# Three low halves of W2 written by an adding DMA, and four key casts moved to GpSimd

## The chip, the cores and the metric

The kernel runs on one core of one Trainium2 chip. The metric is the device time of one execution in microseconds (us); the median of three runs before the change is 792.12 us, the lowest 791.73 and the highest 793.36. The engines are called PE (TensorE, matrix products), DVE (VectorE), ACT (ScalarE), POOL (GpSimd) and SP (SyncE, which issues most DMAs). Each works through its own list of instructions in order; an instruction that must wait holds up all that stand behind it on its engine.

## The reference

Block-sparse attention is followed by layer norm and a two-layer network with a residual:

```
scores = q @ k.T / 8                     # 4 batches, 8 heads, 768 positions, 64 per head
scores = where(mask, scores, -1e9)       # mask from blocks of 32: window, edges, sampled blocks
attn   = softmax(scores) @ v
x      = attn, heads side by side        # (4, 768, 512)
xn     = (x - mean) / sqrt(var + 1e-6) * g
out    = x + relu(xn @ W1) @ W2          # W1 512 x 2048, W2 2048 x 512, given as float64
```

## The kernel before

All large products are done in fp16 with each operand split into a high half (the value rounded to fp16) and a low half (what the rounding left, again in fp16). A product is then three: high by high, high by low, low by high. So whatever PE reads has first to be cast (high half) and subtracted (low half) by other engines.

The work goes in 12 units, each a third of a batch (256 positions); a unit has four pairs of heads, so there are 48 segments and 96 score groups of 12 matmuls (function `scores`, L602). Per segment follow the masked maxima on DVE (L611, in pairs), the exponentials on ACT (L625), the normalised high half `ph` on ACT (L688) and its low half `pl` on DVE (L692, after a reciprocal pair L677 and L679), their transposition by DMA, and the product with `v` (L728 to L737). Per unit follow the layer norm (its last step is `xl`, the low half of the normed values, L877), the first layer's 192 products with `w1h`, `w1l` and the second layer's 192 with `w2h`, `w2l` (both in `product`, L313), and the stores: `ot` on DVE (L932), which also frees the bank of accumulators, and an output DMA. The products of the network serve as filler: PE takes them in a fixed order, in between the score groups and the products with `v`. Only in unit 0 does the second layer go chunk by chunk of W2, two banks side by side, since W2 is still being unpacked.

W1 comes in 8 chunks and W2 in 16; `(2, 15)` is W2's last chunk. `loads_w` (L482) handles one chunk: a DMA brings the float64 bits into a raw buffer (W2's last chunks share two buffers, `raw0` and `raw1`, with the raw keys); DVE puts an fp32 number together from them in three steps (`first` L529, `second` L533, `third` L537, or L542 with POOL's addition L547); ACT scales it (L565) and casts the high half (L571); then the low half is made, by POOL's `tensor_sub` (L577), or by DVE for the chunks in LOWDVE (L579). `loads_k` (L351) handles the keys of a pair of heads: DMA L360, cast to the high half `kh` on ACT (L370), low half `kl` on DVE for the first 12 of 16 and on POOL for the last four (L363). `loads_q` copies queries by a DMA that POOL issues (L397), and POOL makes their low half (L400).

The order of each engine's instructions is set by the class `Plan`: every piece of work is a task with an engine, an assumed cost, tasks it comes after, a rank, and buffers it takes and gives back. `run` builds the lists greedily from these numbers, and `lock` keeps DVE's and POOL's tasks apart in its reckoning (on the chip nothing keeps them apart but the semaphores). A changed task can thus change the order of everything planned later.

Of the kernel before, what the change touches and what calls it, by code (L numbers as in the profile page):

```python
# [13 lines left out]
AF = mybir.ActivationFunctionType  # L14
ALU = mybir.AluOpType
# [161 lines left out]
def sparse_attention_moe(  # L177
# [12 lines left out]
    nc = tc.nc  # L190
# [31 lines left out]
    HIGHAT, LOWAT = -3.61, 0.01  # L222
# [2 lines left out]
    LOWDVE = ((2, 2), (1, 1), (2, 11), (1, 7), (2, 4), (2, 6), (2, 3), (1, 0), (2, 9), (2, 13), (1, 6), (1, 2))  # L225
    AVHOLD = 4
    KEEP = 90000.0
    CASTK, CASTQ = 16, 5
    MASKAT = 11.99
    KAT, VAT, QAT = 4.32, 10.55, 11.84  # L230
# [20 lines left out]
    def queue_of(kind):  # L251

        return (nc.gpsimd, "POOL", 900) if kind in POOLQ else (nc.sync, "SP", 580)

    plan = Plan()
    plan.span, plan.hot, plan.cold, plan.deep = 3400.0, 0.85, 0.4, 7000.0
    plan.keep, plan.first = KEEP, 1400.0
    plan.mode, plan.plain = None, PLAIN
# [92 lines left out]
    def loads_k(b, pr, rank, before):  # L351
        idx = b * NPAIR + pr
        o = SimpleNamespace()
        qk = "k" if b else ""

        def raw():
            o.kh = kvp.tile([P, S], F16, tag="kh", name=f"kh{idx}")
            o.kl = kvp.tile([P, S], F16, tag="kl", name=f"kl{idx}")
            o.kr = raw_s[RAWS.index(plan.where("raw", ("k", idx)))][:, 0:S]
            queue_of(qk)[0].dma_start(o.kr, ks[b, pr])  # L360

        def low():
            (nc.vector if idx < KDVE else nc.gpsimd).tensor_sub(o.kl, o.kr, o.kh)  # L363

        o.raw = plan.add(*queue_of(qk)[1:], raw, (before,), rank, 2000, load=1120, order="k",
                         take=(("k", idx), ("raw", ("k", idx), 2 if idx < RAWS_S else 1, RAWS)))
        if idx < RAWS_S:
            rank = 4 * pr + SPLITAT
        if idx < CASTK:
            o.high = plan.add("ACT", 730, lambda: nc.scalar.copy(o.kh, o.kr), (o.raw,), rank)  # L370
        else:
            o.high = plan.add("POOL", 560, lambda: nc.gpsimd.dma_start(o.kh, ks[b, pr]),
                              (o.raw,), rank, 2300, load=1500, order="k")
        e, x = ("DVE", 870) if idx < KDVE else ("POOL", 1640)
        o.low = plan.add(e, x, low, (o.raw, o.high), rank, give=(("raw", ("k", idx)),), lock=True)
        return o
# [105 lines left out]
    def loads_w(kind, i, before, w1done, low_tail):  # L482

        o = SimpleNamespace()
        own = (kind, i)
        qw = "w" if kind == 2 else ""
        if kind == 1:
            fs = slice(i * 2 * P, (i + 1) * 2 * P)
            rank = W1AT[i]
            scale, size, name = SW1, 1.0, "w1"  # L490
            stage = ("hh", "hl")[i] if i < 2 else "w1raw"
            take = ((stage, own),)
        else:
            rank = W2AT[i]
            scale, size, name = SW2, 0.5, "w2"
            stage = "raw"
# [53 lines left out]
        if kind == 2 and i >= 10:  # L550
# [3 lines left out]
            load=2900 * size, take=take, order="w")  # L554
# [20 lines left out]
        def low():  # L575
            if own not in LOWDVE:
                nc.gpsimd.tensor_sub(o.dl, o.src, o.dh)  # L577
            else:
                nc.vector.scalar_tensor_tensor(out=o.dl, in0=o.src, scalar=left, in1=o.dh,  # L579
                                               op0=ALU.mult, op1=ALU.subtract)  # L580

        if own in HIDMA and own in PORC:
            o.high = plan.add("POOL", 560, lambda: nc.gpsimd.dma_start(o.dh, o.src), (d,), rank + HIGHAT,
                              4300, load=2270 * size)
        else:
            o.high = plan.add("ACT", 940 * size + 60, high, (d,), rank + HIGHAT)
        e, x = ("DVE", 1135 * size + 35) if own in LOWDVE else ("POOL", 2020 * size + 140)
        o.low = plan.add(e, x, low, (o.high,), rank + LOWAT, lock=True,
            give=((stage, own),) + ((("wf", own),) if kind == 1 else ()))
# [411 lines left out]
    for rank, kind, x, pr in sorted(order):  # L1001
        if kind == 0:
            kt[x, pr] = loads_k(x, pr, rank, lk)
            lk = kt[x, pr].raw
        elif kind == 1:
            qt[x] = loads_q(x, rank, lq)
            lq = qt[x].raw
            if x == 0:
                iota = plan.add("POOL", 350, lambda: nc.gpsimd.affine_select(
                    ident, ident, pattern=[[-1, P]], compare_op=ALU.not_equal, fill=1.0, base=0,  # L1010
                    channel_multiplier=1), (qt[0].raw,), -5)
        else:
            vt[x, pr] = loads_v(x, pr, rank, lv)
            lv = vt[x, pr].last
# [4 lines left out]
    for i in range(FP):  # L1019
        wo1.append(loads_w(1, i, lw, (), ()))  # L1020
        lw = wo1[-1].load
        if i == 0:
            lw.after += [kt[0, 0].raw, qt[0].raw]
            for x in lw.after[-2:]:
                x.next.append(lw)
                lw.left += 1
    for i in range(FT):
        tails = [x.low for x in wo2[:10]] if i >= 10 else ()
        wo2.append(loads_w(2, i, lw, [x.low for x in wo1], tails))
        lw = wo2[-1].load  # L1030
# [3 lines left out]
    for seg in segs:  # L1034
# [4 lines left out]
        for t in range(TS):  # L1039
            a, b = pair = seg.slots[2 * t : 2 * t + 2]  # L1040
            give, whole = (), seg.i < RAWS_S
            if t == TS - 1:
                give = ((("qr", seg.i), ("raw", ("k", pr))) if whole else (("q", seg.i),)) + ((("k", u.b * NPAIR + pr),)
                                          if LAST[u.b, pr] is seg else ())
# [26 lines left out]
        if seg.early and (seg.i + NPAIR >= len(segs) or not segs[seg.i + NPAIR].early):  # L1071
            rank = seg.slots[0].i + UPS + 1
# [9 lines left out]
    for seg in segs:  # L1082
        n = 2 * seg.i + AVHOLD
# [71 lines left out]
```

## Time and profile before

| | |
|---|---|
| median of three runs | 792.12 us |
| span of the profiled execution | 790.0 us |
| busy: PE | 778.1 us (98%) |
| busy: DVE | 621.5 us (79%) |
| busy: ACT | 509.4 us (64%) |
| busy: POOL | 105.2 us (13%) |
| last matrix product begins | 786.28 us |

The span runs from the first to the last event that the profiler saw on the core; the run's own time is a little longer than the span. No other time of the profiled execution is given. Shares are averages over stages with different limits, so the stretch in question has to be looked at by itself. The profile's timelines give start, length, engine, line, operation, what it writes and reads, and, in brackets, how long the engine sat idle before it and for what.

### The profile page before, as it was taken

To read this page: it belongs to the slowest core of one execution; us is meant where nothing else is said; L and a number is where in the kernel's file an instruction comes from. 1 tells how busy PE (TensorE), PEld (TensorE's weight loads), DVE (VectorE), ACT (ScalarE), POOL (GpSimd) and SP (SyncE) were. 2 spreads that over 40 slices of the span, in tenths; PEclk is the share of its full clock that TensorE was granted. 3 is DMA by queue.
4 is the path that set the end of the run, shared out by engine and by line. 5 is a ranking of instruction groups with operands and counts; after the bars stand their busy time and mean duration, and the time that the engine had idled before them with its cause. 6 is when DMAs were issued, how large, how long until landed. Compare 5 with 4: busy or idle time off the path is not lost.

```text
span 790.0 us, 18464 instructions
## 1 busy us (share of the span) xinstructions
PE 778.1 (98%) x7336; PEld 600.0 (76%) x7336; DVE 621.5 (79%) x1225; ACT 509.4 (64%) x948; POOL 105.2 (13%) x117
## 2 busy tenths in 40 slices
PE   8999999999999999999999999999999999999998
PEld 5655677778777777777777777777777777788887
DVE  6989999988988788989878878888877878854220
ACT  6888876687666667777766766667656657652110
POOL 0444332200101000001011012021000100000000
PEclk9999999999999999999999999999999999999999
DMA  9553545978977688998785787887766656561000
GB/s 324 181 147 109 161 135 153 231 161 164 165 134 129 139 128 162 169 192 157 144 135 124 132 163 132 172 166 156 137 131 112 140 118 110 121 122 25 21 1 27
DMA packets 285638, 109.27 MB, mean 138 GB/s; under 512 B 253808, under 2 KB 277360, under 8 KB 285552
## 3 DMA queue, kind: packets, MB, share of 16 engines
q1 hardware_dynamic: 278544, 104.91, 61.1%
q0 software_dynamic: 6720, 3.08, 3.5%
q8 instruction: 57, 0.93, 0.5%
q14 instruction: 29, 0.24, 0.1%
q10 hardware_dynamic: 288, 0.10, 0.1%
HBM read 42.97 MB, written 6.29 MB: 62 GB/s over the span
## 4 chain that ended last, share of the span: by engine, by line
PE 89%; DVE 6%; ACT 2%; DMA 1%; issue 1%; SPq 1%; POOL 0%; ACTq 0%
PE bank L313 65%; PE ps L602 11%; PE pa L732 7%; PE pa L737 3%; PE pa L728 1%; DVE p L611 1%; DMA w1r<-w 1%; PE bank L640 1%; DVE w2h L533 1%; ACT pt L647 1%; DVE w2h L529 0%; DVE allow L328 0%; DVE w2h L537 0%; ACT p L625 0%; POOL w2h L547 0%
## 5 line engine op out<-in xcount | busy, mean ns | idle before, releaser
L313 PE MATMUL bank<-hh,w2h 128*128 128x256 f16 x768 | 204.5, 273 | 0.0
L313 PE MATMUL bank<-hh,w2l 128*128 128x256 f16 x768 | 204.1, 273 | 0.0
L313 PE MATMUL bank<-hl,w2h 128*128 128x256 f16 x768 | 204.1, 273 | 0.0
L611 DVE CUSTOM_DVE_ANT_1 p<-ps,allow 128x768 f32<-128x768 f32 x184 | 170.1, 951 | 24.0 <-PE ps L602 23.8
L625 ACT ACTIVATE p<-p,st 128x768 f32<-128x768 f32 x184 | 170.5, 928 | 15.7 <-DVE st L611 15.5
L313 PEld LDWEIGHTS <-w2h 128*128 128x128 f16 x1536 | 147.4, 98 | 25.8 <-issue 8.9
L313 PEld LDWEIGHTS <-w1h 128*128 128x128 f16 x1536 | 148.7, 98 | 23.6 <-issue 6.7
L313 PE MATMUL bank<-xh,w1h 128*128 128x256 f16 x768 | 115.4, 273 | 1.4 <-ACT pt L647 1.4
L313 PE MATMUL bank<-xh,w1l 128*128 128x256 f16 x768 | 115.4, 273 | 0.0
L313 PE MATMUL bank<-xl,w1h 128*128 128x256 f16 x768 | 115.3, 273 | 0.0
L916 DVE SCALAR_TENSOR_TENSOR hl<-bank,hh 128x512 f16<-128x512 f32 x96 | 66.2, 689 | 48.5 <-ACT hh L910 47.7
L910 ACT ACTIVATE hh<-bank 128x512 f16<-128x512 f32 x96 | 57.0, 594 | 65.4 <-PE bank L313 64.7
L688 ACT ACTIVATE ph<-p,st 128x768 f16<-128x768 f32 x92 | 83.5, 927 | 19.6 <-issue 8.2
L692 DVE SCALAR_TENSOR_TENSOR pl<-p,st,ph 128x768 f16<-128x768 f32 x92 | 94.3, 1042 | 1.2 <-DMA pt<-pl 1.0
L313 PEld LDWEIGHTS <-w1l 128*128 128x128 f16 x768 | 73.3, 98 | 13.7 <-issue 5.5
L313 PEld LDWEIGHTS <-w2l 128*128 128x128 f16 x768 | 75.0, 98 | 8.9 <-issue 0.2
L732 PE MATMUL pa<-pt,vh 128*64 128x512 f16 x468 | 79.2, 383 | 0.0
L688 ACT ACTIVATE raw<-p,st 128x768 f16<-128x768 f32 x64 | 57.9, 928 | 25.6 <-issue 14.7
L397 POOL DMA_DIRECT2D qh<-q x43 | 24.6, 571 | 333.7 <-PE ps L602 299.7
L692 DVE SCALAR_TENSOR_TENSOR raw<-p,st,raw 128x768 f16<-128x768 f32 x64 | 67.0, 1062 | 0.0
L602 PE MATMUL ps<-kh,qh 64*128 64x512 f16 (+1 forms) x376 | 64.9, 328 | 0.6 <-DVE st L611 0.5
L737 PE MATMUL pa<-pt,vl 128*64 128x256 f16 x468 | 64.6, 273 | 0.0
(125 smaller groups left out, 986.7 us busy)
## 6 DMA issues: line engine op xcount, KB each, us to landing
qr<-q SPq DMA_DIRECT2D x48, 128.0 KB, 3.0
raw<-k SPq DMA_DIRECT2D x16, 384.0 KB, 3.9
vr<-v SPq DMA_DIRECT2D x32, 192.0 KB, 2.9
out<-ot SPq DMA_DIRECT2D x48, 128.0 KB, 1.9
raw<-w SPq DMA_DIRECT2D x11, 512.0 KB, 3.8
w2l<-w SPq DMA_DIRECT2D x4, 1024.0 KB, 8.0
qh<-q POOLq DMA_DIRECT2D x43, 64.0 KB, 3.0
w1r<-w SPq DMA_DIRECT2D x2, 1024.0 KB, 8.3
```

What stands on the lines that cost most here:

```text
L313: nc.tensor.matmul(dst, w, x, start=start, stop=stop, skip_group_check=True)
L397: o.high = plan.add("POOL", 560, lambda: nc.gpsimd.dma_start(o.qh, qs[u.b, pr, u.c]), (o.raw,), rank, 2300, load=600, order="q")
L533: nc.vector.scalar_tensor_tensor(out=o.wf, in0=o.raw[:, :, 1], scalar=-0x40000000, in1=o.wf, op0=ALU.bitwise_and, op1=ALU.bitwise_or)
L602: nc.tensor.matmul(s.ps[:, lo:hi], x[rows, s.qs], y[rows, lo:hi], start=n == 0, stop=n == len(terms) - 1)
L611: nc.vector.tensor_tensor_reduce(out=s.p.rearrange(blk, k=BLK), in0=s.ps[:, 0:S].rearrange(blk, k=BLK), in1=bias, scale=-0.125, scalar=3.0 ...
L625: nc.scalar.activation(s.p, s.p, AF.Exp, bias=s.st[:, j : j + 1], scale=-1.0, accum_out=total)
L688: nc.scalar.activation(s.ph, s.p, AF.Copy, scale=s.r)
L692: nc.vector.scalar_tensor_tensor(out=s.pl, in0=s.p, scalar=s.r, in1=s.ph, op0=ALU.mult, op1=ALU.subtract)
L732: nc.tensor.matmul(seg.pa[half[hh], 0 : 2 * CH], vo.vh[:, hh, t, :], pts[keys[hh]][:, t].rearrange("p i n -> p (i n)"), start=t == 0, stop ...
L737: nc.tensor.matmul(seg.pa[half[hh], 0:CH], vo.vl[:, hh, t, :], pts[keys[hh]][:, t, 0, :], start=False, stop=t == KT - 1, skip_group_check= ...
L910: nc.scalar.activation(u.hh[:, f : f + 2, :].rearrange("p f n -> p (f n)"), bank[plan.where("bank", own)], AF.Relu)
L916: nc.vector.scalar_tensor_tensor(out=u.hl[:, f : f + 2, :].rearrange("p f n -> p (f n)"), in0=bank[plan.where("bank", own)], scalar=0.0, i ...
```

## The change

For three chunks of W2 the low half is made in another way. Before, it was one subtraction, fp32 value minus high half. Now an engine first writes the negated high half into the low half's place (chunk 5: DVE, chunk 14: POOL, chunk 15: ACT), and then a DMA that POOL issues adds the fp32 chunk onto it. And the keys of the last batch (numbers 12 to 15) are cast to their high half by POOL's copy, where ACT did it.

```diff
+    LOWDMA = {(2, 5): "DVE", (2, 14): "POOL", (2, 15): "ACT"}
+    CASTPOOL = 12
...
-        if idx < CASTK:
+        if idx >= CASTPOOL:
+            o.high = plan.add("POOL", 1000, lambda: nc.gpsimd.tensor_copy(o.kh, o.kr), (o.raw,), rank,
+                              lock=True)
+        elif idx < CASTK:
             o.high = plan.add("ACT", 730, lambda: nc.scalar.copy(o.kh, o.kr), (o.raw,), rank)
...
+        def minus():
+            if LOWDMA[own] == "ACT":
+                nc.scalar.activation(o.dl, o.dh, AF.Copy, scale=-1.0)
+            elif LOWDMA[own] == "DVE":
+                nc.vector.tensor_scalar(out=o.dl, in0=o.dh, scalar1=-1.0, scalar2=None,
+                                        op0=ALU.mult)
+            else:
+                nc.gpsimd.tensor_scalar(out=o.dl, in0=o.dh, scalar1=-1.0, scalar2=1.0,
+                                        op0=ALU.mult, op1=ALU.mult)
...
+        if own in LOWDMA:
+            e = LOWDMA[own]
+            n = plan.add(e, {"DVE": 400, "ACT": 1000, "POOL": 1200}[e] * size, minus, (o.high,),
+                         rank + LOWAT, lock=e != "ACT")
+            o.low = plan.add("POOL", 560, lambda: nc.gpsimd.dma_start(o.dl, o.src, accum_op=ALU.add),
+                             (n,), rank + LOWAT, 4300, load=2270 * size, give=((stage, own),))
+            return o
```

Because the tasks and their assumed costs differ, the plan puts the work in another order from about 100 us on. Line numbers grow by 5 up to `loads_w` and by up to 22 behind it.

On POOL, the two subtractions of chunks 14 and 15 (the third and fourth row here; the first is that of an earlier chunk), before:

```order
L577 TENSOR_TENSOR w2l<-raw_116,w2h 128x512 [waits Activation_49]
L397 DMA qh_1835<-q 128x256 [waits PE_49]
L577 TENSOR_TENSOR w2l<-raw_116,w2h 128x512 [waits Activation_49]
L577 TENSOR_TENSOR w2l<-raw_115,w2h 128x512 [waits Activation_49]
L400 TENSOR_TENSOR ql_118<-qr_1834,qh_1835 128x256 [waits DMAHW2_49,DMASW2_49,PE_49]
```

and the same place in the changed kernel, where L594 is the negation for chunk 14 and the two rows L606 are the adding DMAs of chunks 14 and 15:

```order
L402 DMA qh_1821<-q 128x256 [waits PE_49]
L594 TENSOR_SCALAR w2l<-w2h 128x512 [waits Activation_49]
L405 TENSOR_TENSOR ql_118<-qr_1820,qh_1821 128x256 [waits DMAHW0_49,DMASW3_49,PE_49]
L606 DMA w2l<-raw_115 128x512 [waits Pool_49]
L606 DMA w2l<-raw_116 128x512 [waits Activation_49]
```

Two subtractions went; a negation and two DMAs stand in their place, chunk 14's behind the queries' low half, chunk 15's behind a wait for ACT's negation.

On DVE, the rows around `xl` up to the last unpacking step of chunk 15 (the last row; its raw buffer is `raw_115`), before:

```order
L692 SCALAR_TENSOR_TENSOR pl<-p_124,st_1552,ph 128x768
L863 SCALAR_TENSOR_TENSOR xc_1578<-xc_1578,g_sb,rs_1732 128x256
L677 TENSOR_SCALAR st_1727<-st_1727 128x2
L679 RECIPROCAL st_1727<-st_1727 128x2
L529 TENSOR_SCALAR raw_116<-raw_116 128x512
L877 TENSOR_TENSOR xl_1776<-xc_1578,xh_1775 128x1024
L533 SCALAR_TENSOR_TENSOR raw_116<-raw_116 128x512
L529 TENSOR_SCALAR raw_115<-raw_115 128x512
L537 SCALAR_TENSOR_TENSOR raw_116<-raw_116 128x512
L533 SCALAR_TENSOR_TENSOR raw_115<-raw_115 128x512
L437 SCALAR_TENSOR_TENSOR vl_199<-vr_1_1486,vh_198 128x384
L537 SCALAR_TENSOR_TENSOR raw_115<-raw_115 128x512
```

In the changed kernel `xl` is followed by the low half of chunk 13 and the last step of chunk 14, and then, up to chunk 15's last step (its buffer is now `raw_116`), by:

```order
L714 SCALAR_TENSOR_TENSOR pl<-p_123,st_1574,ph 128x768
L714 SCALAR_TENSOR_TENSOR pl<-p_124,st_1574,ph 128x768
L633 ISA p_123,st_1875<-ps_1786,allow 128x768
L633 ISA st_1875 128x1
L633 ISA p_124,st_1875<-ps_1787,allow 128x768
L633 ISA st_1875 128x1
L534 TENSOR_SCALAR raw_116<-raw_116 128x512
L699 TENSOR_SCALAR st_1719<-st_1719 128x2
L701 RECIPROCAL st_1719<-st_1719 128x2
L538 SCALAR_TENSOR_TENSOR raw_116<-raw_116 128x512
L442 SCALAR_TENSOR_TENSOR vl_199<-vr_1_1492,vh_198 128x384
L542 SCALAR_TENSOR_TENSOR raw_116<-raw_116 128x512
```

Two `pl` that stood ahead of `xl` and a pair of masked maxima now stand between `xl` and that step.

On PE, the first product with chunk 15's low half (`w2l`), before:

```order
L313 LDWEIGHTS w2h
L313 MATMUL bank_100<-hl_1175,w2h 128x256
L313 LDWEIGHTS w2h
L313 MATMUL bank_100<-hl_1175,w2h 128x256
L313 LDWEIGHTS w2l [waits Pool_49]
L313 MATMUL bank_100<-hh_1169,w2l 128x256
```

and in the changed kernel:

```order
L624 LDWEIGHTS ql_119
L624 MATMUL ps_1992<-kh_300,ql_119 128x256
L624 LDWEIGHTS ql_119
L624 MATMUL ps_1993<-kh_300,ql_119 128x256
L315 LDWEIGHTS w2l [waits DMASW5_49]
L315 MATMUL bank_99<-hh_1169,w2l 128x256
```

A score group stands right ahead of it now (one more stands further up), and the product waits for the adding DMA where it waited for POOL.

## Rows read from the trace of the kernel before

**Rows 1.** The page's head: span of the profiled execution.
```profile
span 790.0 us, 18464 instructions
```
**Rows 2.** By stretch: length, busy PE, PEld, DVE, ACT, POOL; granted clock, DMA share, GB/s.
```profile
100.00:165.00 65.00, 65.00 (x617) 51.81 (x612) 62.33 (x129) 45.56 (x89) 17.87 (x17) 1.00 0.66 167
165.00:786.50 621.50, 621.50 (x5963) 487.00 (x5960) 469.44 (x932) 382.27 (x687) 54.42 (x69) 1.00 0.67 128
```
**Rows 3.** Timeline of PE, 140 to 142.5 us: start, length, engine, line, operation.
```profile
140.60 0.38 PE L313 MATMUL bank<-hh,w2l 128*128 128x256 f16 x2
140.82 0.38 PE L313 MATMUL bank<-hh,w2h 128*128 128x256 f16 x2
141.14 0.39 PE L602 MATMUL ps<-kh,qh 64*128 64x512 f16 x2
...
142.22 0.39 PE L313 MATMUL bank<-hl,w2h 128*128 128x256 f16 x2
```
**Rows 4.** Tile `kl`: POOL's subtractions; ns min/median/max, first and last start.
```profile
L363 POOL TENSOR_TENSOR kl<-raw,kh x4: 1642/1646/2095, 476.3 to 524.9; 128x768 f16<-128x768 f32 x4
```
**Rows 5.** Chain of waits, 520 to 526 us: first score group of the last batch.
```profile
523.17 1.08 PE ps L602 x12
```
**Rows 6.** Tile `w2l`: PE's reads of it, and POOL's subtraction for chunk 5.
```profile
L313 PE MATMUL bank<-hh,w2l x768: 272/273/282, 129.9 to 786.3; 128*128 128x256 f16 x192
...
L577 POOL TENSOR_TENSOR w2l<-w2h x1: 1423/1423/1423, 104.1 to 104.1; 128x512 f16<-128x512 f32 x1
```
**Rows 7.** Timeline of PE: first low products of chunk 14 and of chunk 15.
```profile
151.83 0.38 PE L313 MATMUL bank<-hh,w2l 128*128 128x256 f16 x2
...
153.14 0.38 PE L313 MATMUL bank<-hh,w2l 128*128 128x256 f16 x2
```
**Rows 8.** Timeline of POOL: the low halves of chunks 14 and 15.
```profile
148.82 2.65 POOL L577 TENSOR_TENSOR w2l<-raw,w2h 128x512 f16<-128x512 f32 x2 [5.77 <-ACT w2h L571]
```
**Rows 9.** Timeline of DVE, 143 to 154 us.
```profile
143.36 0.15 DVE L677 TENSOR_SCALAR st<-st 128x2 f32<-128x2 f32 x1
...
143.97 1.22 DVE L877 TENSOR_TENSOR xl<-xc,xh 128x1024 f16<-128x1024 f32 x1
145.11 0.69 DVE L533 SCALAR_TENSOR_TENSOR raw<-raw 128x512 int32<-128x512 int32 x1
...
147.25 0.55 DVE L437 SCALAR_TENSOR_TENSOR vl<-vr,vh 128x384 f16<-128x384 f32 x1
147.72 0.68 DVE L537 SCALAR_TENSOR_TENSOR raw<-raw 128x512 int32<-128x512 int32 x1
148.32 1.01 DVE L692 SCALAR_TENSOR_TENSOR pl<-p,st,ph 128x768 f16<-128x768 f32 x1
149.25 0.95 DVE L611 CUSTOM_DVE_ANT_1 p<-ps,allow 128x768 f32<-128x768 f32 x1
...
151.00 1.29 DVE L692 SCALAR_TENSOR_TENSOR pl<-p,st,ph 128x768 f16<-128x768 f32 x1
...
153.63 0.74 DVE L932 SCALAR_TENSOR_TENSOR ot<-bank,xT 128x256 f32<-128x256 f32 x2
```
**Rows 10.** Timeline of ACT, 147 to 150 us: scaling and casts of chunks 14 and 15.
```profile
147.30 0.92 ACT L688 ACTIVATE ph<-p,st 128x768 f16<-128x768 f32 x1
148.13 0.60 ACT L571 CAST w2h<-raw 128x512 f16<-128x512 f32 x1
148.63 0.62 ACT L565 ACTIVATE raw<-raw 128x512 f32<-128x512 f32 x1
149.29 0.62 ACT L571 CAST w2h<-raw 128x512 f16<-128x512 f32 x1
```
**Rows 11.** Tile `qh`: its 43 POOL-issued copies, issue to landing.
```profile
DMA to landing us min/median/max: 2.3/3.0/7.1
```
**Rows 12.** The same, 140 to 170 us alone: two copies.
```profile
DMA to landing us min/median/max: 3.8/4.3/4.8
```
**Rows 13.** DMA issues: the copy inside the on-chip memory; median to landing.
```profile
w1h<-w2h POOLq DMA_DIRECT2D x1, 256.0 KB, 3.6
```

## The prediction

> **What bounds the kernel now.** I first read the page's head [rows 1], then the table of busy time by stretch [rows 2]: from 100 us to the last product at 786.5 us the matrix engine (PE) is busy 65.00 of 65.00 and 621.50 of 621.50 us at a granted clock of 1.00. It never waits there. VectorE (DVE) is busy 62.33 of 65.00 us between 100 and 165 us, and 469.44 of 621.50 us after that. Two things follow. Work that the change takes off ScalarE (ACT), GpSimd (POOL) or DVE after 100 us gives nothing back, since nothing on PE waits for it. And any wait that the change puts on PE after 100 us is paid in full: there is no idle time later to absorb it. Up to 100 us the orders of the engines are the same with and without the change, so the early stalls stay. So the sum has two terms: PE's own work, and new PE waits, which can only lie where a changed low half is first used.
>
> **The change part by part.** *PE's own work.* The count of matmuls is the same. The new order changes PE's tile shape five times more, all before chunk 15's low half is first used. One change costs 0.10 us: the score group starts 0.32 us after the product before it, where product follows product by 0.22 [rows 3]. Five make **0.5 us**.
>
> *Keys of the last batch.* Four casts leave ACT for POOL. I price one at 1.65 us or less, the time of POOL's two-input subtraction on the same tile; POOL does the first at 476.3 us, and PE first reads that batch at 523.17 us [rows 4, 5], 45 us later even with the cast ahead of it. POOL is busy 54.42 us in 621.50 [rows 2]. Cost: nothing; with the cover gone it would be at most 4 × 1.65 = 6.6 us.
>
> *Chunk 5.* Its subtraction ran on POOL at 104.1 us, and no second-stage low half is read by PE before 129.9 us [rows 6]. A negation on DVE (under 0.7 us, the length of a two-input step of that size) and a transfer fit into 25 us. Cost: nothing.
>
> *Chunk 15, where I put the price.* Before, PE reads its low half first at 153.14 us [rows 7], and POOL's two subtractions (148.82 + 2.65 = 151.47 us [rows 8]) are done 1.7 us ahead. Now three things are later.
>
> First, the unpacking on DVE. Between `xl` and the last unpacking step before stood five rows, 145.11 to 147.72 = 2.61 us. In the new order there stand: the low half of chunk 13 and chunk 14's last step (0.60 each), two `pl` (0.93 each), a pair of masked maxima (149.25 to 151.00 = 1.75), a first step with a reciprocal pair (143.36 to 143.97 = 0.61), a second step (0.60) and one `vl` (0.47): 6.49 us [rows 9]. That is 3.88 more, so the last step starts at 147.72 + 3.88 = 151.60 and ends 0.68 later, at 152.28. This takes `xl` at its old time: two `pl` (1.9 us) that stood ahead of it stand behind it now, but it waits for four ACT casts behind the same exponentials. So `xl` may lie up to 1.9 us earlier, the lower bound of this step.
>
> Second, ACT. Before, from the end of the step (148.40) to the end of the cast (149.91) went 1.51 us. Now a `ph` (0.83, 147.30 to 148.13) lies between, and the negation (0.50, the cast's own pitch) behind [rows 10]: 152.28 + 1.51 + 0.83 + 0.50 = 155.12.
>
> Third, the transfer with addition, which no row shows. Below: 2.3 us, the fastest of 43 small POOL-issued copies; above: 7.1, the slowest of them. The nearest rows: 3.8 to 4.8 us for the two of those copies in just this stretch, and 3.6 for a copy inside the on-chip memory of twice the elements [rows 11 to 13]. I take 4.8, since this transfer also reads what it writes: it lands at 159.92 (bounds, from 155.12: 157.4 and 162.2).
>
> [...] The measured copies of this stretch, with a quarter of the bytes, took 3.8 and 4.8, so I follow those.
>
> When does PE want it? Its order has exactly two more score groups ahead of that product and the five shape changes: 153.14 + 2 × 0.98 + 0.50 = 155.60 (a group is 1.08 us with its change [rows 3]). The groups are work drawn forward, not added. So PE waits 159.92 − 155.60 = **4.3 us**.
>
> *What the wait covers.* Chunk 14: PE wants it at 151.83 plus one group and a change or two, 153.1 [rows 7]. Its last step ends about 145.11 + 0.60 + 0.68 = 146.4, two ACT operations 1.2 later, POOL's negation (0.6 to 1.3; I take 1.0) and a small subtraction next, then the transfer, landing at 154 to 154.7: up to 1.6 us late. PE then comes to chunk 15 at 157.2 at the latest, still before 159.9, so this adds nothing. The keys of chunk 5's raw buffer now wait for that transfer; their low half stands on DVE ahead of the two stores (`ot`) that free PE's next bank. DVE gets there like this: from the start of its next row, 152.20, all that stood between 148.32 and 154.37 (two `pl`, a maxima pair, four small steps, two stores: 6.05 us) comes again, plus two reciprocal pairs (0.3 each), two more `pl` and the keys' low half (0.93 each): 152.20 + 6.05 + 0.6 + 2.8 = 161.6 [rows 9]. PE wants the bank 32 products of 0.109 us, 3.5 us, after chunk 15's first low product: at 163.4 in my sum. Covered; without the transfer's wait it would not be (below).
>
> Sum: 0.5 + 4.3 = **+4.8 us** on the profiled span of 790.0, which makes 794.8. The span is 2.1 us under the median of the three runs, 792.12; I keep that distance: **796.9 us**.
>
> **The rivals.**
>
> *(a) No measurable loss.* A difference under 0.2% (1.6 us) can't be told from none. If `xl` comes 1.9 us earlier and the transfer takes its lower bound, it lands at 155.12 − 1.9 + 2.3 = 155.5, before PE asks. DVE would free the bank at 159.7 for 159.1 wanted. What is left is 0.5 for the shape changes and 0.2 to 0.6: 792.8 us. For it: three POOL subtractions are gone, and a `pl` beside one took 1.29 us where others took 1.01 [rows 9], so DVE may run a little faster. [...] Against it: the copies in this stretch took 3.8 and 4.8.
>
> *(b) DVE, not the transfer, sets the end.* With a landing before about 158, PE loses little there, but `ot` comes at 161.6 for a bank wanted at 155.60 + 3.5 = 159.1: 2.5 us, and 0.5 for the shapes: 795.1 us. It decides once the landing is earlier than 161.6 − 3.5 = 158.1.
>
> *(c) A later transfer.* At the upper bound of 7.1 it lands at 162.2, and PE loses 6.6 + 0.5: 799.2 us; with the issue itself held up a `pl` or two on top (0.93 each), 801. For it: POOL's own copies spread to 7.1, DVE is 96% busy in this stretch, and the transfer engines are already 0.66 busy in it [rows 2]. [...]
>
> *(d) The key casts stall PE.* It needs POOL 40 us late; nothing in the profile speaks for it. Up to 803.5.
>
> **How the numbers follow.** Forecast 0.54, (a) 0.14, (b) 0.18, (c) 0.12, (d) 0.02. The likeliest gives 796.9. The range reaches from (b) less the unknown of `xl`, 793.8, to a transfer just above its bound, 800.4. It leaves out (a), (d) and half of (c)'s upper part, some 0.2. Faster by over 0.2%: 0.04, since PE after 100 us has no idle time to give back and only its early stalls could shrink; within 0.2%: 0.12, nearly all of (a); slower: 0.84.
>
> **What would show it.** PE with idle time in one place, 150 to 165 us, on the first low product of chunk 15, released by the accumulating transfer (forecast, c), or a few us later by `ot` (b); no idle time elsewhere after 100 us; the landing of these transfers near 4.8 us; 261 shape changes; chunk 15's last unpacking step near 151.6; key casts of 1.65 us or less with nobody waiting for them. A landing of 3 us or less, `xl` near 142, or idle time on PE at 136 or 523 us would make the prediction wrong. So would a span that shrinks with PE still fully busy.

## The result, and the profile after

The changed kernel takes 800.15 us (median of three runs, 798.71 to 802.43), where 792.12 was measured before: the ratio is 1.0105, with a 95% interval of 1.009 to 1.012. That is 8.0 to 8.3 us slower; the forecast was 4.8 us slower, 796.9. So the sign and the place of the longest wait were right and the size was not. The time lies at the upper end of the forecast's range (793.8 to 800.4) and nearest to rival (c), whose late landing the trace does not have (below).

The page of the profiled execution, which was the shortest of the three (their spans were 796.8, 798.4 and 799.5 us), and PE's waits after 100 us, by what was waited for (total us, times, longest):

```profile
span 796.8 us, 18457 instructions
```

```profile
PE bank L315 <- DMA w2l<-raw: 3.3, 2, 2.6
PE ps L624 <- DVE st L633: 0.5, 1, 0.5
PE pa L754 <- DMA pt<-pl: 0.2, 1, 0.2
```

Before there was no such wait [rows 2]. Where they stand on PE's timeline (start, length, then idle time before it and its releaser):

```profile
153.46 0.39 PE L315 MATMUL bank<-hh,w2l 128*128 128x256 f16 x2 [0.69 <-DMA w2l<-raw]
...
155.84 0.37 PE L624 MATMUL ps<-kh,qh 64*128 64x512 f16 x1 [0.51 <-DVE st L633]
...
159.59 0.51 PE L315 MATMUL bank<-hh,w2l 128*128 128x256 f16 x2 [2.61 <-DMA w2l<-raw]
...
161.17 1.06 PE L315 MATMUL bank<-xh,w1h 128*128 128x256 f16 x4
162.02 1.06 PE L315 MATMUL bank<-xh,w1l 128*128 128x256 f16 x4
162.88 0.73 PE L315 MATMUL bank<-xl,w1h 128*128 128x256 f16 x4
163.45 0.60 PE L315 MATMUL bank<-xh,w1h 128*128 128x256 f16 x4
```

The first is chunk 14's low half, the third chunk 15's. Behind the third, four products take 0.85 us (161.17 to 162.02) where they take 0.44 elsewhere. The windows say why (length; busy PE, PEld, DVE, ACT, POOL; granted clock; DMA share; GB/s):

```profile
160.00:161.00 1.00, 1.00 (x7) 0.67 (x6) 0.47 (x1) 0.63 (x1) 0.00 (x0) 0.50 1.59 180
161.00:163.00 2.00, 2.00 (x11) 1.40 (x10) 1.70 (x4) 0.23 (x1) 0.00 (x0) 0.50 1.25 267
163.00:164.00 1.00, 1.00 (x11) 0.84 (x10) 1.00 (x3) 0.88 (x2) 0.00 (x0) 0.93 1.06 205
164.00:166.00 2.00, 2.00 (x21) 1.80 (x19) 2.00 (x5) 1.80 (x3) 0.00 (x0) 1.00 1.30 338
```

After its idle time of 2.61 us PE ran at a granted clock of 0.50 until about 163.1 us: the 20 products from 159.59 to 163.45 took 3.86 us and would have taken 20 × 0.109 = 2.18. So the span's 6.8 us read like this: 3.8 us of waits up to 159.6 and 0.3 at about 183 us, 1.7 of halved clock, and 1.0 for the rest (the forecast had 0.5 for shape changes). A single execution also differs from another before the change can act: up to 100 us the orders are equal, and yet the same query copy goes out 0.6 us earlier here (second row) than in the trace before (first row), so that after it 7.4 us are lost.

```profile
100.75 0.57 POOL L397 DMA_DIRECT2D qh<-q  x1 [1.12 <-PE ps L602]
100.15 0.73 POOL L402 DMA_DIRECT2D qh<-q  x1 [2.42 <-PE ps L624]
```

The experiments show that this reading is only half of the cause. What they turn on is on DVE:

```profile
143.17 1.23 DVE L899 TENSOR_TENSOR xl<-xc,xh 128x1024 f16<-128x1024 f32 x1 [0.24 <-ACT xh L895]
...
150.80 0.69 DVE L542 SCALAR_TENSOR_TENSOR raw<-raw 128x512 int32<-128x512 int32 x1
...
160.53 1.02 DVE L714 SCALAR_TENSOR_TENSOR pl<-p,st,ph 128x768 f16<-128x768 f32 x1 [3.46 <-DMA pt<-pl]
...
163.03 0.95 DVE L365 TENSOR_TENSOR kl<-raw,kh 128x768 f16<-128x768 f32 x1
163.89 0.75 DVE L954 SCALAR_TENSOR_TENSOR ot<-bank,xT 128x256 f32<-128x256 f32 x2
```

`xl` came 0.8 us earlier than before [rows 9], chunk 15's last unpacking step 3.1 us later (forecast 3.9); counted from the earlier start of this trace, 0.2 earlier and 3.7 later. But at 157 us DVE, which had 9.40 busy us in 150 to 160 before, sat idle for 3.46 us: the buffer of the next `pl` was still being read by a transposition. The stores `ot`, which free PE's bank, queue behind it: they end at 164.6 us, where the forecast had 161.6. PE comes to that bank at 164.8, behind the 32 products that begin at 159.59, and so does not wait; at the full clock, 3.5 us for these products, it would have come at 163.1 and waited.

### The profile page after: what moved, and what is told of

It reads as the page before. It is cut to its first block, busy times and chain, and to the rows that moved or that the text cites. A ratio compares the mean times of both kernels' runs of the same rounds, so it can differ in the third digit from the quotient of the medians.

```text
span 796.8 us, 18457 instructions
## 1 busy us (share of the span) xinstructions
PE 781.8 (98%) x7336; PEld 601.9 (76%) x7336; DVE 620.5 (78%) x1226; ACT 506.5 (64%) x945; POOL 109.0 (14%) x122
## 4 chain that ended last, share of the span: by engine, by line
PE 84%; DVE 7%; DMA 4%; ACT 3%; issue 1%; SPq 0%; DVEq 0%; ACTq 0%
PE bank L315 59%; PE ps L624 10%; PE pa L754 7%; PE pa L759 3%; PE pa L750 2%; DMA raw<-k 2%; DMA pt<-pl 2%; PE bank L662 1%; DVE p L633 1%; DVE pl L714 1%; DVE kl L365 1%; ACT pt L669 1%; ACT p L647 0%; PE pa L775 0%; DMA out<-ot 0%
## 5 line engine op out<-in xcount | busy, mean ns | idle before, releaser
L714 DVE SCALAR_TENSOR_TENSOR pl<-p,st,ph 128x768 f16<-128x768 f32 x92 | 91.5, 1016 | 5.1 <-DMA pt<-pl 4.6
L315 PEld LDWEIGHTS <-w2l 128*128 128x128 f16 x768 | 75.1, 98 | 12.7 <-DMA w2l<-raw 4.0
```

The source lines that it names most:

```text
L315: nc.tensor.matmul(dst, w, x, start=start, stop=stop, skip_group_check=True)
L714: nc.vector.scalar_tensor_tensor(out=s.pl, in0=s.p, scalar=s.r, in1=s.ph, op0=ALU.mult, op1=ALU.subtract)
```

## The experiments

Ratios are against the kernel before, run on the same chip beside it, with their 95% intervals. Line numbers in the rows are those of each kernel.

| run | kernel | ratio | us more |
|---|---|---|---|
| e1 | key casts alone | 0.9996 (0.9985 to 1.0007) | −0.3 |
| e12 | old order, chunk 5 by DMA | 1.0004 (0.9995 to 1.0014) | 0.3 |
| e5 | old order, chunks 14, 15 by DMA | 1.0065 (1.0044 to 1.0086) | 5.1 |
| e4 | new order, chunks 14, 15 subtracted | 1.0090 (1.0074 to 1.0107) | 7.1 |
| | the changed kernel | 1.0105 (1.009 to 1.012) | 8.3 |
| e6 | changed, wait filled with products | 1.012 (1.010 to 1.014) | 9.5 |
| e7 | changed, stores first | 1.0111 (1.0098 to 1.0125) | 8.8 |
| e8 | e7, wait filled | 1.0127 (1.0108 to 1.0146) | 10.1 |
| e9 | e4, stores first | 1.0096 (1.008 to 1.0113) | 7.6 |
| e10 | e9, more `pl` buffers | 1.0091 (1.0078 to 1.0105) | 7.2 |
| e11 | e7, more `pl` buffers | 1.0103 (1.0088 to 1.0119) | 8.2 |
| e14 | e10, more `ph` buffers | 1.0090 (1.0075 to 1.0105) | 7.1 |
| e15 | e11, more `ph` buffers | 1.0098 (1.0081 to 1.0114) | 7.8 |
| e16 | e14, six loads on POOL | 1.0152 (1.0138 to 1.0166) | 12.0 |
| e3 | own order, chunk 5 by DMA, key casts | 1.0173 (1.0158 to 1.0188) | 13.7 |
| e13 | own order, nothing but a plan cost changed | 1.0051 (1.0039 to 1.0064) | 4.0 |

"us more" is the ratio less one times 792. The first theory was that of the forecast, with the clock added: the adding transfers make the loss.

**e1, the key casts alone.**

```diff
-    LOWDMA = {(2, 5): "DVE", (2, 14): "POOL", (2, 15): "ACT"}
+    LOWDMA = {}
```

> LOWDMA is empty: only the four key casts on GpSimd are left of the change. Theory 1 (the whole loss comes from the adding transfers at 150 to 165 us, as waits of PE and as a lower granted clock behind them): within 0.8 us of before, no wait of PE after 100 us, key casts of 1.65 us or less that nobody waits for. Rival (the casts delay PE late in the kernel): 2 us or more slower than before, with PE idle between 515 and 560 us.

As expected: no time lost and no wait of PE after 100 us. The casts took 0.82 to 1.32 us each (0.82 to 1.62 in the changed kernel):

```profile
L372 POOL CAST kh<-raw x4: 822/959/1318, 472.7 to 524.7; 128x768 f16<-128x768 f32 x4
```

**e12, chunk 5 alone in the old order.**

```diff
+            if own == (2, 5):
+                nc.vector.tensor_scalar(out=o.dl, in0=o.dh, scalar1=-1.0, scalar2=None, op0=ALU.mult)
+                nc.gpsimd.dma_start(o.dl, o.src, accum_op=ALU.add)
...
```

> The plan and order of the kernel before, with chunk 5's low half alone made by DVE's negation and the adding DMA in the place of GpSimd's subtraction. Theory (a transfer with 25 us of cover costs nothing by itself; what the run with chunk 5 alone lost came from its other order): within 0.8 us of before. Rival (an adding DMA disturbs the stage wherever it stands): 2 us or more slower.

As expected. Its transfer went out at 104.5 us and took 4.1 us to land; PE first reads a low half of W2 at 129.1, 20 us later.

**e5, the old order with the transfers of chunks 14 and 15.** Here ACT negates both.

```diff
+            if kind == 2 and i >= 14:
+                nc.scalar.activation(o.dl, o.dh, AF.Copy, scale=-1.0)
+                nc.gpsimd.dma_start(o.dl, o.src, accum_op=ALU.add)
...
```

> The plan and order of the kernel before, keys as before, but chunks 14 and 15 get ACT's negation and the adding DMA in the place of GpSimd's subtraction. Theory 1: chunk 14's transfer lands about 154.4 us where PE wants it at 151.8 (wait 2.6), chunk 15's about 156.4 (0.7 more), and the clock falls behind the wait (1.7): 5 us slower than before. Rival 2 (the order): within 1 us of before.

5.1 us is the number expected, but it is made up in another way: one wait for chunk 14 of 4.5 us (2.6 expected), since the landing took longer, and none for chunk 15. PE's one wait after 100 us, the landing of the two transfers, and the clock behind them:

```profile
PE bank L313 <- DMA w2l<-raw: 4.5, 1, 4.5
```

```profile
DMA to landing us min/median/max: 5.6/5.7/5.9
```

```profile
156.00:158.00 2.00, 2.00 (x10) 1.45 (x11) 0.00 (x0) 0.18 (x1) 0.00 (x0) 0.50 1.05 352
```

So the two late adding transfers by themselves cost about what the forecast gave the whole change (5.1, interval 3.5 to 6.8, against 4.8), though the wait stands at chunk 14 and not at chunk 15.

**e4, the new order without the two transfers.** The plan is that of the changed kernel; only what is issued differs, and chunk 5's transfer and the key casts stay.

```diff
         def minus():
+            if i >= 14:
+                return
...
-            o.low = plan.add("POOL", 560, lambda: nc.gpsimd.dma_start(o.dl, o.src, accum_op=ALU.add),
+            o.low = plan.add("POOL", 560, lambda: nc.gpsimd.tensor_sub(o.dl, o.src, o.dh) if i >= 14 else
+                             nc.gpsimd.dma_start(o.dl, o.src, accum_op=ALU.add),
```

> The plan, and so the order of all engines, is that of the changed kernel, but for chunks 14 and 15 the negation is not issued and GpSimd does the old subtraction where the adding DMA stood. Theory 1 (the transfer's latency): chunk 15's low half is ready about 154.7 us, PE comes at 155.6 to 156.5, so no wait there, no fall of the clock; 0.5 to 1.5 us slower than before, from five more shape changes and one wait for the masked maxima. Rival 2 (the new order itself, with the masked maxima and pl ahead of the last unpacking step, makes the loss): 4 us or more slower than before.

The first theory fell here: 7.1 us are lost with no late transfer at all, so the order alone loses no less than the transfers alone (the intervals, 5.9 to 8.5 and 3.5 to 6.8, overlap), and both together (8.3) far less than their sum. PE's waits, and the stretch behind them, in which the granted clock fell here too (0.66 on average):

```profile
PE bank L315 <- DVE ot L957: 3.0, 1, 3.0
PE ps L627 <- DVE st L636: 1.3, 2, 0.8
```

```profile
165.00:170.00 5.00, 5.00 (x33) 3.48 (x32) 3.49 (x9) 3.77 (x7) 0.66 (x1) 0.66 1.11 248
```

PE waits for the bank that `ot` frees, and DVE is late for the same reason as in the changed kernel:

```profile
160.21 1.02 DVE L717 SCALAR_TENSOR_TENSOR pl<-p,st,ph 128x768 f16<-128x768 f32 x1 [2.46 <-DMA pt<-pl]
```

**e6, the wait filled.** 22 products of constants in front of chunk 15's first low product; they are read by nobody.

```diff
+                            if (f, pair, n) == (FT - 1, 0, 2):
+                                free = plan.sets["bank"].free
+                                filler(next(p for p in free if free[p] is not None), 22)
```

> The changed kernel, with 22 products of constants (128x256, into the free bank, read by nobody) on PE between the last score group and the first product with chunk 15's low half: they take some 2.4 us of the 2.6 us that PE sat idle there. Theory 1, second part (PE's granted clock of 0.50 from 160 to 163.4 us comes from its idling just before): the clock stays at 1.00, the waiting ends at the same time, and the kernel is 1.7 us faster than the changed one. Rival 3 (the clock falls for another reason, so that PE's work there is merely slow): no gain, or as much as 0.5 us lost.

The clock stayed at 1.00, as the theory had it, where the changed kernel had 0.50 in these 2 us:

```profile
161.00:163.00 2.00, 2.00 (x21) 1.79 (x20) 1.71 (x4) 0.08 (x1) 0.00 (x0) 1.00 1.25 247
```

and yet nothing was won (9.5 us, interval 7.9 to 11.1). PE came to the next bank sooner and waited there, and for transpositions:

```profile
PE pa L754 <- DMA pt<-pl: 1.7, 3, 0.7
PE bank L315 <- DVE ot L954: 1.4, 1, 1.4
```

So the halved clock cost the changed kernel nothing that this run gives back: the wait for `ot` stood behind it in any case. Hence the second theory: two waits, the transfer and `ot`, each hiding the other.

**e7, e9, e8: the stores first.** Unit 0's first two `ot` are issued on DVE ahead of the `pl` that waits (in e7 for the changed kernel, in e9 for e4, in e8 with e6's products).

```diff
+                            if (f, pair, n) == (FT - 1, 0, 2):
+                                early[0](now=True)
+                                early[1](now=True)
+                                while pend:
+                                    pend.pop(0)()
...
```

The lines left out hold these two `ot`, and the first of the two `pl`, back from their old place; `pend` has that `pl`.

> The changed kernel with one difference in order: unit 0's first two stores (ot) stand on DVE ahead of the pl, the reciprocal pair, the pl and the keys' low half that stood ahead of them. New theory (two waits one behind the other: chunk 15's transfer, and then the bank that ot frees only at about 164.5 us, because DVE waits 3.5 us for a pl buffer with ot queued behind it; each hides part of the other): the bank is free by 161 us, the wait for the transfer (2.6) and the halved clock behind it (1.7) stay: some 6 us slower than before, 1.5 to 2.5 us faster than the changed kernel. Rival (the transfer alone makes the loss): as slow as the changed kernel, 8 us.

> The new order with GpSimd's subtraction for chunks 14 and 15 (no negation, no adding DMA there), and unit 0's first two stores ahead on DVE. New theory: neither of the two waits is left, and no fall of the clock; what stays are two waits for the masked maxima (1.3) and the shape changes (0.5): 1.5 to 2.5 us slower than before. Rival 2 (the new order is slow for other reasons too): 4 us or more slower than before.

> The changed kernel with the first two stores ahead on DVE, and the 22 constant products in the wait for chunk 15's transfer. New theory: the stores no longer hold PE back, so the full clock that the products keep now shows: 1.7 us faster than the kernel with the stores ahead alone, about 4 us slower than before. Rival (what PE wins there is lost in a third wait): no faster than that kernel.

All three missed. The wait for `ot` is gone in each, and no time with it: 8.8, 7.6 and 10.1 us. In e7 the edit moves DVE's idle time rather than removing it: `ot` now stands first and waits itself for PE's products, and the `pl` behind it begins at 161.15 (160.53 in the changed kernel).

```profile
160.48 0.76 DVE L961 SCALAR_TENSOR_TENSOR ot<-bank,xT 128x256 f32<-128x256 f32 x2 [2.61 <-PE bank L315]
```

In e9 PE waits one step on, at the next bank, which `hl` frees behind the same late DVE rows:

```profile
PE bank L315 <- DVE hl L946: 2.2, 1, 2.2
```

**e10, e11: other buffers for two `pl`**, in a raw buffer's half that nobody uses then, so that DVE doesn't wait.

```diff
-                s.pl = half_of(1, plan.where("pl", s.i))
+                s.pl = (half_of(43 - s.i, 2) if s.i in (42, 43) else
+                        half_of(1, plan.where("pl", s.i)))
...
```

> The new order with subtractions and stores first, as the run before it, and two pl of segment 10 are written into the unused half of a raw buffer, so that DVE doesn't wait for the transpositions of the pl before them. Third theory (in the new order DVE is late by its waits for pl buffers, 1.6 to 3.5 us, and every bank that it frees behind them comes late; moving the stores only moved PE's wait from ot to the next hl): DVE gains 1.6 us, PE's wait of 2.2 us for hl falls to 0.6 or less and the clock doesn't fall behind it, so some 2.5 to 4 us slower than before, against 7.6 without the buffers. Rival (the loss of the new order isn't in this chain): as slow as without the buffers, 7 us or more.

> The changed kernel with the stores first and the same two pl buffers. Third theory (two chains, the adding transfer with the clock behind it, and DVE's lateness, end within 2 us of each other; only with both relieved does the loss go): the transfer's wait (2 to 2.6), the halved clock (1.7) and the smaller waits stay: 5 to 7 us slower than before. Rival (the pl buffers are the only cause): 4 us or less slower than before.

Both missed: 7.2 and 8.2 us. In e10 the DVE idle time before `pl` is gone, and `hl` is late by another way: it needs ACT's relu copy `hh`, which queues behind two `ph` that wait for transpositions. PE's wait, and ACT's:

```profile
PE bank L315 <- DVE hl L947: 2.6, 1, 2.6
```

```profile
162.59 0.94 ACT L715 ACTIVATE ph<-p,st 128x768 f16<-128x768 f32 x1 [2.37 <-DMA pt<-ph]
164.45 0.93 ACT L715 ACTIVATE ph<-p,st 128x768 f16<-128x768 f32 x1 [0.92 <-DMA pt<-ph]
165.29 0.58 ACT L941 ACTIVATE hh<-bank 128x512 f16<-128x512 f32 x1
```

**e14, e15: other buffers for two `ph` as well.**

```diff
+                s.ph = (half_of(45 - s.i, 3) if s.i in (44, 45) else
+                        half_of(0, plan.where("ph", s.i)))
...
```

> New order, subtractions for chunks 14 and 15, stores first, two pl of segment 10 in other buffers, and now also two ph of segment 11 in another unused half of a raw buffer, so that ACT doesn't wait for transpositions with the relu copy (hh) behind. Fourth theory (the new order is late through the two-deep ph and pl buffers, whose transpositions stand in SyncE's queue): hh at about 162 in place of 165.3 us, hl at 163.7, PE's wait of 2.6 us there falls to 0.5: 3 to 5 us slower than before, against 7.2 without the ph buffers. Rival (the next wait takes over once more and in full): 7 us slower.

> The same with chunks 14 and 15 by the adding DMA, so the changed kernel with stores first and the pl and ph buffers relieved. Fourth theory: what stays is the wait for the transfer (2 to 2.6 us) and what hangs on it: 5 to 6 us slower than before, as the transfers cost in the old order (5.1). Rival: 8 us slower, as the changed kernel.

7.1 and 7.8 us: the rival's number. `hh` came at 162.41 as wanted, `hl` at 164.08, and PE waits for the transpositions themselves, at the products with `v` (e14):

```profile
PE pa L764 <- DMA pt<-raw: 2.0, 2, 1.0
PE pa L764 <- DMA pt<-pl: 1.6, 2, 1.0
```

**e16, six loads taken off SyncE's queue** (two of keys, three of `v`, one of queries, issued by POOL).

```diff
-            queue_of(qk)[0].dma_start(o.kr, ks[b, pr])
+            (nc.gpsimd if idx in (5, 6) else queue_of(qk)[0]).dma_start(o.kr, ks[b, pr])
...
```

> As the run with pl and ph buffers and subtractions, but six loads of 150 to 164 us (two of keys, three of v, one of queries) are issued by GpSimd in place of SyncE, about 3 us of SyncE's issue time. Fifth theory (SyncE's queue is the last resource in the new order): the transpositions of segment 11 go out 2 us earlier, PE's waits for them (2.0 and 1.6 us) fall to 1 or less together, and the kernel is 4 to 5.5 us slower than before in place of 7. Rival (the new order has yet another limit behind it, or the loads come too late on GpSimd): 6.5 us or more slower.

12.0 us, worse. The first transposition out of a raw buffer went out at 160.43 us, sooner than in e14 (164.12), but the transpositions of 150 to 170 us now took 2.8 to 12.7 us to land, median 6.9 (in e14 2.5 to 4.6, median 3.8):

```profile
DMA to landing us min/median/max: 2.8/6.9/12.7
```

PE's one long wait, with the clock at 0.50 behind it, is for a product that reads such a transposition; the profile puts it down to ACT, which had itself waited 5.1 us for keys that POOL loads:

```profile
PE pa L765 <- ACT p L651: 6.1, 1, 6.1
```

So freeing the queue in this way wins nothing: the landings took longer, and why is not shown. As the run changed both, the queue and the landings, it does not show that the queue by itself is no limit. A further hint, and no proof, is in the DMA share (second number from the end) of e14,

```profile
145.00:150.00 5.00, 5.00 (x48) 4.49 (x46) 5.00 (x8) 1.55 (x3) 1.86 (x2) 1.00 0.50 138
150.00:155.00 5.00, 5.00 (x54) 3.18 (x53) 4.62 (x12) 4.62 (x9) 0.54 (x2) 1.00 0.46 113
160.00:165.00 5.00, 4.70 (x44) 4.07 (x42) 4.73 (x10) 2.91 (x4) 0.00 (x0) 1.00 1.28 219
165.00:170.00 5.00, 3.00 (x29) 1.78 (x29) 1.80 (x4) 3.75 (x7) 0.66 (x1) 1.00 1.29 254
```

beside the same stretches of the kernel before:

```profile
145.00:150.00 5.00, 5.00 (x51) 4.17 (x50) 5.00 (x9) 3.11 (x5) 1.18 (x1) 1.00 1.03 228
150.00:155.00 5.00, 5.00 (x55) 3.37 (x50) 4.61 (x12) 3.15 (x7) 2.82 (x3) 1.00 0.96 197
160.00:165.00 5.00, 5.00 (x49) 3.85 (x47) 4.41 (x9) 3.96 (x10) 0.57 (x1) 1.00 0.96 154
165.00:170.00 5.00, 5.00 (x49) 3.78 (x48) 4.66 (x8) 4.12 (x8) 0.66 (x1) 1.00 0.70 184
```

In the new order the transfers rest at 145 to 155 us and crowd at 160 to 170. A single transposition is hardly slower for it: of those issued from 150 to 170 us the median took 3.8 us to land in e14 and 3.4 before, the longest 4.6 in both. Keys 5 and 6 are loaded into chunk 14's and 15's raw buffers: before, both loads went out from 150.86 us, in the changed kernel at 154.83 and 161.75. It is not the release of the buffer that sets this time. In e4 POOL is done with chunk 15's at 155.74 us (first row), and the load into it goes out at 161.77, right behind a transposition in SyncE's list:

```profile
154.26 1.48 POOL L608 TENSOR_TENSOR w2l<-raw,w2h 128x512 f16<-128x512 f32 x1 [4.46 <-ACT w2h L576]
160.50 1.21 SPq L723 DMA_TRANSPOSE pt<-ph  x1
161.77 0.57 SPq L362 DMA_DIRECT2D raw<-k  x1
```

In e14 ACT's list then stands still for these keys, with exponentials behind the cast:

```profile
166.25 0.83 ACT L375 CAST kh<-raw 128x768 f16<-128x768 f32 x1 [3.26 <-DMA raw<-k]
```

**e3 and e13: is the order's loss peculiar to this change?** e3 leaves chunks 14 and 15 to the subtraction and plans anew; e13 changes no instruction, only the cost that the plan assumes for chunk 5's subtraction.

```diff
-    LOWDMA = {(2, 5): "DVE", (2, 14): "POOL", (2, 15): "ACT"}
+    LOWDMA = {(2, 5): "DVE"}
```

> Only chunk 5's low half by the adding DMA, and the key casts on GpSimd; chunks 14 and 15 are subtracted as before. By the forecast's reading chunk 5's transfer has 25 us of cover: within 0.8 us of before, no wait of PE after 100 us. Rival (any adding DMA in this stage reorders or delays something that PE waits for): 1.6 us or more slower.

```diff
+        if own == (2, 5):
+            x += 300
```

> The kernel before, its instructions unchanged in kind and number; only the plan's assumed cost of GpSimd's subtraction for chunk 5 is 300 ns higher, which gives another order from about 105 us on. Theory (the planner's orders differ by several us among themselves, so that a changed cost alone can lose as much as the change did): 2 us or more slower than before, with a wait of PE after 100 us. Rival (the order matters only where a transfer is late): within 0.8 us of before.

e3 missed: 13.7 us, the most of all, but not by a transfer. It has no wait of note at 150 to 165 us, and 7.9 us of waits between 200 and 300 us, where its order puts the casts of `xh` too late (the granted clock was 0.99 on average from 200 to 700 us, 1.00 in each stretch from 140 to 200):

```profile
PE bank L315 <- ACT xh L895: 7.9, 4, 5.4
```

e13, as its theory had it, loses 4.0 us by a changed number in the plan. From 150 to 175 us its PE waits 2.1 us in all, in pieces of 0.6 or less. Its span is 4.3 us longer than before; 0.9 of them lie ahead of any change of order (the product that begins at 98.88 us before begins at 99.81 here), and the remaining 1.3 I did not trace. With e12 this settles chunk 5: the transfer is free, the order that comes with it may not be.

## Why the prediction was right or wrong

**The bound, the keys and chunk 5** were right: no time was won by relief of any engine after 100 us, and the key casts and chunk 5's transfer cost nothing by themselves (e1, e12). For chunk 5 "cost: nothing" holds for the instruction, not for the plan that it changes (e3).

**Chunk 15's transfer** came close: the negation ended at 154.16 (forecast 155.12), POOL's issue began 0.3 later, the landing took 5.1 (4.8), and PE's product started at 159.59 (159.92). That the end is only 0.3 off is in part luck: with this trace's start 0.6 us early, the negation was 0.4 early and the issue and the landing 0.6 late. The wait in front of it was 2.6 and not 4.3, since PE came there 1.4 us late, having waited 0.69 for chunk 14 and 0.51 for the maxima; chunk 14's delay was absorbed as the text said. The reason given for 4.8, that the transfer also reads what it writes, no run shows: none has the same transfer without the addition. Nor was the landing of one adding transfer a fixed time: 4.1 us for chunk 5's in e12, 3.5 for it and 4.9 and 5.1 for the other two in the changed kernel, 5.6 and 5.9 in e5, where the two went out 1.2 us apart.

**The step that failed** is the premise of the sum, that new waits of PE "can only lie where a changed low half is first used", and with it "What the wait covers", with its "Covered", and rival (b). That step took DVE's rows up to `ot` as a string of durations, 152.20 to 161.6, because in the trace of before DVE is 96% busy there. In the new order that string has a hole of 3.46 us, a wait for a `pl` buffer; I priced the moved rows and not the buffers that they take, nor SyncE's transpositions that free these. So `ot` freed the bank at 164.6 us, not 161.6, where PE at its full clock would have come at 163.1: not covered. Rival (b) was given 3.0 us where e4, in which no transfer is late, measured 7.1. The wait for `ot` itself was 3.0 there, near the 2.5 of (b); what the sum put at nothing were 1.3 us of waits for the masked maxima and a clock of 0.66 on average over 5 us behind the wait, some 1.7 us.

The measured time alone would speak for rival (c), 799.2 us, a landing after 7.1 us. The landing took 5.1, so that nearness is chance. That a `pl` or two holds up the issue itself, the step from 799.2 to 801, no run shows: chunk 15's began 0.3 us after the negation and took 0.86. And the range was wrongly added: its lower end is said to be (b) less the 1.9 us of `xl`, which is 793.2 and not 793.8. The sign "no idle time elsewhere after 100 us" also failed: PE waited 0.5 us for the maxima at 155.8 and 0.2 for a transposition at 183.

Behind this stands a wrong frame. The sum looked at the new order only for what stands ahead of chunk 15's product. The order was itself the larger change: two score groups drawn forward bring eight transpositions with them and put the stores and the key loads into another sequence, and e4 shows that this alone loses 7.1 us, e13 that even a changed cost in the plan can lose 4.0. **The clock** was missing from the sum too (1.7 us in the trace), but e6, where it stayed at 1.00, won nothing back.

**What stays open.** In e4, e9, e10 and e14 one wait after the other was taken away, and the loss stayed at 7.1 to 7.6 us: PE waited for `ot`, then `hl` by DVE, then `hl` by ACT, then the transpositions; in e4 and e9 the clock fell behind the wait (0.66 on average from 165 to 170 us), in e10 and e14 it stayed at 1.00. So it is none of these waits alone. e16 does not settle whether SyncE's list is the limit, since the landings changed with it. That the crowded transfers of 160 to 170 us are the limit fits the DMA shares, but the transpositions' landing times hardly do, and no run took the crowding away and nothing else. The late place of the two key loads in SyncE's list is a candidate that no run tested by itself.

## What to carry to other kernels

Where a planner writes the order, price a changed order as a change of its own: run the new order with the old instruction, and the old order with the new one, before explaining anything by the instruction. A chain read as a sum of durations must also be read for the buffers that each row takes and for who gives them back. Two late chains that end together don't add up, and removing either shows nothing; the sum of PE's waits in one trace is then no account of causes.

## What the runs showed of the hardware

The halved clock did not follow from the length of the last idle time alone: it fell behind idle times of 2.61 us in the changed kernel (0.50 from 160 to 163 us), 3.04 in e4 (0.50 from 166 to 168) and 2.18 in e9 (0.66 on average from 165 to 170), and in e10 it stayed at 1.00 through one of 2.60. All four had two shorter ones ahead (0.69 and 0.51, 0.78 and 0.51, 0.78 and 0.50, 0.81 and 0.50). No run shows what sorts them. An adding DMA of one chunk took 3.5 us (chunk 5, changed kernel) to 5.9 (e5) from issue to landing. POOL's issue of an adding DMA took 0.86 to 1.10 us on its timeline (1.10 in e6), against 0.56 to 0.73, median 0.57, for its 43 plain copies of queries in the changed kernel. POOL's cast of 128 x 768 from fp32 to fp16 took 0.82 us at best, as ACT's (median 0.83), and up to 1.62 in the changed kernel.
